# A new order for the first two batches of an attention and max-out kernel, and new PSUM bank rings

## The chip, the core and the metric

The kernel runs on one core of a Trainium2 chip, in one launch. The metric is device microseconds (us) from its start to its end; smaller is better. Times before: 151.38 us, the median of three runs (151.37 to 151.61).

## The reference

```python
# x (8, 8, 512, 64), state (8, 8, 32, 64); B, H, S, D and 32 state rows
a      = softmax(x @ state^T / 8, over the state rows)
xread  = a @ state
a2     = softmax(state @ x^T / 8, over the 512 tokens)
sread  = a2 @ x
t      = concat([xread, sread], axis=2) -> (8 * 544, 512)     # heads side by side
out    = max(t @ w1, t @ w2) @ w_out                           # 512 -> 1024 -> 512
```

All inputs and the output are float32 in DRAM; the kernel computes in bfloat16 with float32 sums in PSUM.

## The kernel before, in words

Rewriting. `max(h1, h2) = h2 + relu(h1 - h2)`, so with `wd = w1 - w2` the output is `t @ (w2 @ w_out) + relu(t @ wd) @ w_out`. The product `w2 @ w_out` is called `wwo`; the kernel makes it once (`wq`, from transposed `w2t`, which comes from `w2` steps, and `wo`). Since xread is `a @ state`, the state is multiplied into the weights first: `SW[b]` is the block-diagonal state (`sbd`) of batch b times `wd` (columns 0 to 1023, in pieces of 128 numbered 0 to 7) and times `wwo` (pieces 8 to 11). These products (`sw`, line 326) use the array in tiles of 64 rows by 32 columns. The attention weights, transposed (`aT`), are then multiplied with `SW`. The state reads (`sr`, line 296) use the array in tiles of 128 by 32. Everything else uses it whole. Going from one tiling to another is what "a change of tiling" means below.

Steps of one batch, by their names in the order: `ldx` loads x (two halves of 512 KB), `ce` casts it to bf16 (`xe`), `xt` transposes it on the array (later batches: `cb` casts to `xb`, and `xtd` transposes by DMA), `sc` gives the scores, their eviction is an exponential (`e`), `nmr` sums and inverts, `nmm` multiplies (`a`), `at` transposes `a` on the array (later `atd`, by DMA), `sr` and `srt` read the state side, `sw` makes `SW`, `l1.b.f` is the product with `wd`, evicted by a relu to `r` (eight pieces f), and the output of 128 tokens by 512 columns is summed from eight `l2p` products with `wo` and two `l2o` products with `aT`; `l2` is all ten together. `store` writes a batch (1 MB). `S` and `S7` transpose the state of batch 0 and of batches 1 to 7 into `sbd`. `cw2`, `cwo`, `sub` turn float32 weight pieces into bf16 `w2b`, `wo`, `wd`. `idle.n.512` are n products of zeros that only keep the array busy.

What sets the order. There is no scheduler at work: in manual schedule each engine runs its instructions in program order, and semaphores make it wait for data and for PSUM banks. The string `ORDER` at the top is that program order up to the end of batch 1 (with the first steps of batch 2). A token `name>V`, `>A`, `>P` is a step on DVE, ACT or POOL (with a digit before it: one half of the eviction), `name:k` is a step of TensorE into PSUM bank k (two digits for `sw`: two banks), and names without either are DMA issues on SP's queue, all of them in one row. Behind it a loop over b = 2 to 6 does, for batch b, the eight `l1`, the scores of batch b + 1, two output tiles, `SW` and `sr` of batch b + 1, and two more tiles; then a tail does batch 7, the 256 state-side tokens (`m1`, `m2`), and the last stores.

In the loop and the tail banks come from rings: `bank("r")` walks through six banks for products and scores, `bank("a")` through two for output tiles; in the tail ring a has all eight.

Staging. Float32 loads go into ten buffers of 1 MB (`h8`): `w1`, `w2`, `w_out` in two halves each, four batches of x; output tiles and later batches reuse them in turn. `xt`, `e`, `a`, `SW`, `r` have two buffers, `aT` three.

Of the kernel before, what the change touches and what calls it, by code (L numbers as in the profile page):

```python
# [45 lines left out]


# [1 line left out]
def kernel(  # L49
# [10 lines left out]
    B, H, S, D = x.shape  # L60
# [17 lines left out]
    at = ctx.enter_context(tc.tile_pool(name="at", bufs=2))  # L78
# [67 lines left out]
    def load_w(w, src, f, n):  # L146
        lo, hi = f * 128, (f + n) * 128
        h, o = lo // 512, lo // 512 * 512
        nc.sync.dma_start(out=half(w, h)[:, :, lo - o:hi - o], in_=src[:, lo:hi].rearrange("(i p) f -> p i f", p=128))  # L149
# [168 lines left out]
    def sw_mm(b, lo, hi, rings="rr"):  # L318
        if b not in SW:
            SW[b] = big.tile([128, 2, WC], BF16, tag="sw", name="sw")  # L320
        pg = [bank(r) for r in rings]
        n = hi - lo
        for i in range(4):
            for g in range(2):
                rhs = wd[64 * g:64 * g + 64, i, lo:hi] if hi <= FF else wwo[64 * g:64 * g + 64, i, lo - FF:hi - FF]
                nc.tensor.matmul(pg[g][32 * i:32 * i + 32, 0:n],  # L326
                                 sbd[64 * g:64 * g + 64, b, i, 32 * g:32 * g + 32], rhs, start=True, stop=True)
# [178 lines left out]
    def l2_mm(b, c, ring):  # L506
# [215 lines left out]
```

## Time and profile before

| | |
|---|---|
| median of three runs | 151.38 us |
| the profiled execution's own time | 151.53 us |
| its span (first to last instruction) | 149.7 us |
| busy: TensorE, DVE, ACT, POOL | 141.2, 80.9, 72.3, 49.8 us |
| DMA | 29.08 MB, mean 194 GB/s; some 11 MB of it are the loads of weights, state and four batches that the order begins with |
| end of the written order on TensorE | 55.57 us after the span's start |
| one batch in the loop | 13.85 us |

A row of the profile in order of time has the start and length in us, the engine, the line, the operation, the tiles written and read, the shape, the count, and, in brackets, how long the engine was idle before it and what ended that. PE is TensorE, DVE VectorE, ACT ScalarE, POOL GpSimd, SPq the queue from which DMAs are issued. The chain of waits follows back from the last instruction what released each step.

### The profile page before, as it was taken

The numbers are of one execution on the slowest core, as the hardware profiler recorded it, in microseconds if no ns is written. First come the engines' busy times: TensorE is split into PE (matmuls) and PEld (weight loads), VectorE is DVE, ScalarE is ACT, GpSimd is POOL, SyncE is SP. The second block draws the span as 40 slices with busy tenths as digits, with TensorE's granted clock in tenths as the row PEclk, the third lists the DMA queues.
The fourth block names the chain that finished last, engine by engine and source line by source line (L and its number), as shares of the span: only waits on it lengthen the run. The fifth ranks groups of instructions, "written<-read, shape, count | busy, mean of one in ns | idle before, by whom it ended". The sixth has DMA issues, their size and how long they took to land.

```text
span 149.7 us, 3138 instructions
## 1 busy us (share of the span) xinstructions
PE 141.2 (94%) x1253; PEld 69.2 (46%) x1253; DVE 80.9 (54%) x164; ACT 72.3 (48%) x140; POOL 49.8 (33%) x73
## 2 busy tenths in 40 slices
PE   6698999898999999999999999999999999999990
PEld 2354454353454445444534454454445444754460
DVE  4369364578676108663757385467627485632100
ACT  4298766655899217153713644072537045510121
POOL 3135210483995032652392349055600500000000
PEclk9999999999999999999999999999999999999999
DMA  3999999999207998776949586977306072102442
GB/s 77 364 363 362 359 366 265 328 348 210 54 4 142 235 344 315 162 155 224 311 91 264 223 236 115 273 292 142 74 0 280 0 208 103 44 0 74 118 167 78
DMA packets 35374, 29.08 MB, mean 194 GB/s; under 512 B 19900, under 2 KB 32444, under 8 KB 34588
## 3 DMA queue, kind: packets, MB, share of 16 engines
q1 hardware_dynamic: 35356, 28.84, 65.4%
q8 instruction: 11, 0.18, 0.6%
q14 instruction: 7, 0.06, 0.2%
HBM read 15.20 MB, written 8.91 MB: 161 GB/s over the span
## 4 chain that ended last, share of the span: by engine, by line
PE 75%; DMA 9%; SPq 5%; issue 5%; DVE 3%; POOL 1%; ACT 1%; ACTq 0%; POOLq 0%
PE bank L371 31%; PE bank L353 17%; PE bank L366 8%; DMA h<-in_moe_w_dram 8%; PE bank L326 4%; PE bank L498 3%; SPq L149 3%; PE bank L400 2%; PE bank L410 2%; PE bank L247 2%; PE bank L296 2%; DVE sbd L101 1%; SPq L153 1%; DMA out_dram<-h 1%; PE bank L408 1%
## 5 line engine op out<-in xcount | busy, mean ns | idle before, releaser
L371 PE MATMUL bank<-wo,r 128*128 128x512 bf16 (+1 forms) x232 | 53.1, 372 | 0.0
L99 ACT COPY h<-bank 128x512 f32<-128x512 f32 (+1 forms) x19 | 10.8, 569 | 51.0 <-PE bank L371 50.9
L371 PEld LDWEIGHTS <-r 128*128 128x128 bf16 x232 | 22.7, 98 | 25.7
L353 PE MATMUL bank<-aT,sw 128*128 128x512 bf16 x128 | 29.9, 379 | 0.0
L344 DVE TENSOR_SCALAR r<-bank 128x512 bf16<-128x512 f32 x28 | 19.2, 690 | 14.6 <-PE bank L353 13.2
L265 POOL TENSOR_TENSOR a<-e,er 128x512 bf16<-128x512 bf16 (+1 forms) x17 | 16.3, 980 | 26.5 <-ACT e L255 14.2
L342 ACT ACTIVATE r<-bank 128x512 bf16<-128x512 f32 x36 | 21.1, 605 | 7.2 <-PE bank L353 6.8
L101 DVE CAST sw<-bank 128x512 bf16<-128x512 f32 (+1 forms) x22 | 13.5, 649 | 12.5 <-PE bank L326 12.4
L103 POOL CAST xb<-h 128x1024 bf16<-128x1024 f32 x12 | 12.4, 1040 | 22.7 <-issue 15.6
L103 POOL CAST xe<-h 128x512 bf16<-128x512 f32 x26 | 15.0, 613 | 11.7 <-DMA h<-in_x_dram 11.5
L353 PEld LDWEIGHTS <-sw 128*128 128x128 bf16 x128 | 11.9, 98 | 13.6 <-issue 0.5
L366 PE MATMUL bank<-sw,aT 128*128 128x512 bf16 (+1 forms) x58 | 16.9, 373 | 0.0
L99 ACT CAST sw<-bank 128x512 bf16<-128x512 f32 (+1 forms) x30 | 15.4, 574 | 2.8 <-PE bank L326 2.8
L101 DVE COPY h<-bank 128x512 f32<-128x512 f32 x14 | 9.4, 668 | 12.7 <-PE bank L371 12.1
L261 DVE TENSOR_REDUCE sums<-e 128x16 f32<-128x512 bf16 (+1 forms) x18 | 10.9, 604 | 3.1 <-ACT e L255 3.0
L255 ACT ACTIVATE e<-bank 128x512 bf16<-128x512 f32 (+1 forms) x18 | 9.4, 549 | 3.6 <-PE bank L247 3.0
L498 PE MATMUL bank<-wo,r 128*128 128x512 bf16 x32 | 8.9, 380 | 0.0
L445 PE MATMUL bank<-wo,w2t 128*128 128x512 bf16 x32 | 8.1, 380 | 0.0
L453 PE MATMUL bank<-wz 128*128 128x512 bf16 x14 | 6.6, 558 | 1.2 <-DVE ones L457 1.2
L326 PE MATMUL bank<-wd,sbd 64*32 64x512 bf16 (+1 forms) x144 | 6.0, 359 | 1.2 <-DVE wd L434 1.2
L247 PEld LDWEIGHTS <-xt 128*128 128x128 bf16 x128 | 5.4, 101 | 3.3 <-ACT xt L99 0.6
L366 PEld LDWEIGHTS <-aT 128*128 128x128 bf16 x58 | 4.9, 98 | 4.1
(80 smaller groups left out, 118.2 us busy)
## 6 DMA issues: line engine op xcount, KB each, us to landing
h<-in_x_dram SPq DMA_DIRECT2D x16, 512.0 KB, 6.7
out_dram<-h SPq DMA_DIRECT2D x6, 1024.0 KB, 4.2
h<-in_moe_w_dram SPq DMA_DIRECT2D x8, 512.0 KB, 10.0
h<-in_moe_w_out_dram SPq DMA_DIRECT2D x4, 512.0 KB, 10.6
out_dram<-h SPq DMA_DIRECT2D x2, 512.0 KB, 3.8
out_dram<-h SPq DMA_DIRECT2D x3, 256.0 KB, 2.1
out_dram<-rs SPq DMA_DIRECT2D x8, 64.0 KB, 1.7
sf<-in_state_dram SPq DMA_DIRECT2D x2, 224.0 KB
```

Of the source, the lines that this page charges most:

```text
L99: nc.scalar.copy(o, i)
L101: nc.vector.tensor_copy(o, i)
L103: nc.gpsimd.tensor_copy(o, i)
L261: nc.vector.tensor_reduce(s_, e_view(b, k0, kn), axis=AXX, op=ALU.add)
L265: (nc.gpsimd if eng == "P" else nc.vector).tensor_mul(e_view(b, k0, kn, "a"), e_view(b, k0, kn), d_(b)["er"][:, :, k0:k0 + kn].unsqueeze(3 ...
L326: nc.tensor.matmul(pg[g][32 * i:32 * i + 32, 0:n], sbd[64 * g:64 * g + 64, b, i, 32 * g:32 * g + 32], rhs, start=True, stop=True)
L342: recent["A"] = nc.scalar.activation(out=o, in_=p, func=ACTF.Relu)
L344: nc.vector.tensor_scalar(o, p, scalar1=0.0, scalar2=None, op0=ALU.max)
L353: nc.tensor.matmul(p, SW[b][:, g, f * 128:(f + 1) * 128], AT[b][:, g].rearrange("p c t -> p (c t)"), start=(g == 0), stop=(g == 1))
L366: nc.tensor.matmul(p[:, lo:hi], AT[b][:, g, c, :], SW[b][:, g, FF + lo:FF + hi], start=(start and g == 0), stop=(stop and g == 1))
L371: nc.tensor.matmul(p[:, lo:hi], R[b][:, f, c * 128:(c + 1) * 128], wo[:, f, lo:hi], start=(start and j == 0), stop=(stop and j == len(fs) ...
L498: nc.tensor.matmul(p, R[b][:, j, c * 128:(c + 1) * 128], wo[:, j, :], start=first(key), stop=last(key, j == f + n - 1))
```

## The change

It has three parts. First, `ORDER` is another one: the same steps, with one product more among the idle ones (15 in place of 14), in another sequence on each engine, with other engines for some evictions and casts, and other banks. The loads start with x of batch 0 and then the state; of the weights the pieces 6 and 7 come ahead of 2 to 5, and `w1` 2 and 3 last; x of batch 1 follows `S7`. On the array `S7` and batch 1's `xt` stand later, `sw` groups stand next to each other more often, and `sr.1` next to `sr.2`. `store.0` is issued ahead of `xtd.3`. Second, ring r is banks 5, 7, 6, 1, 2, 4 and ring a is 3, 0. Third, in the tail ring a is the old ring a followed by ring r, written as a sum.

```diff
--- before.py
+++ after.py
@@ -16,32 +16,32 @@
 
 
 ORDER = """
-ldS.0.1 ldx.0.1 ldx.0.0 ldw2.0.2 ldw1.0.2 ldwo.0.2 ldw2.2.2 ldw1.2.2 ldwo.2.2 ldw2.6.2 ldw2.4.2 ldwo.6.2
-ldwo.4.2 ldw1.4.2 ldx.1.1 ldS7 ldx.1.0 ldw1.6.2 ldx.2.1 ldx.2.0 ldx.3.1 ldx.3.0 idle.4.512:0 cS.0.1>V S.0.1:0
-idle.3.512:1 S.0.1>0V S.0.1>1A ce.0.2>V ce.0.3>A xt.0.2.1:1 xt.0.3.1:2 xt.0.2.1>V idle.1.512:3 xt.0.3.1>V
-sc.0.2.1:3 sc.0.2.1>A sc.0.3.1:4 idle.1.512:5 ce.0.1>P ce.0.0>A nmr.0.2.1>V sc.0.3.1>A xt.0.1.1:5 xt.0.0.1:6
-nmr.0.3.1>V xt.0.1.1>A idle.1.512:7 xt.0.0.1>A nmm.0.2.1>V nmm.0.3.1>P sc.0.1.1:7 sc.0.1.1>A sc.0.0.1:0
-idle.1.512:1 nmr.0.1.1>V sc.0.0.1>A cw2.0.1>P cw2.1.1>A sr.0:1 nmr.0.0.1>V nmm.0.1.1>P w2.0.2:2 sr.0>V
-idle.1.512:3 nmm.0.0.1>P w2.0.2>A sub.1.1>V srt.0:3 at.0.0:4 at.0.1:5 at.0.0>A idle.2.512:6 sub.0.1>V
-cwo.0.1>A cwo.1.1>P at.0.1>V sw.0.0.2:67 srt.0>A wq.1.0.2:0 sw.0.0.2>0A sw.0.0.2>1V wq.2.0.2:1 cw2.2.1>V
-cw2.3.1>A l1.0.0:2 l1.0.1:4 l1.0.0>A w2.2.2:5 l1.0.1>A wq.0.0.2:3 sub.2.1>V w2.2.2>A l2p.0.3.0.2:6 sub.3.1>V
-l2p.0.2.0.2:7 wq.3.0.2:2 cwo.2.1>P cwo.3.1>A sw.0.2.2:45 wq.0.2.2 sw.0.2.2>0V sw.0.2.2>1A wq.2.2.2 cw2.7.1>A
-l1.0.2:5 l1.0.3:4 cw2.6.1>A l1.0.2>V wq.1.2.2 l1.0.3>A wq.3.2.2 cw2.4.1>P cw2.5.1>V w2.6.2:5 l2p.0.3.2.2
-w2.6.2>V w2.4.2:4 cwo.7.1>A l2p.0.2.2.2 cwo.6.1>V w2.4.2>A l2p.0.1.0.2:5 wq.2.6.2 cwo.4.1>V cwo.5.1>A wq.0.6.2
-l2p.0.1.2.2 wq.2.4.2 wq.3.6.2 sub.4.1>V wq.2>A wq.0.4.2 sub.5.1>V wq.1.4.2 wq.0>A wq.1.6.2 ce.1.2>P ce.1.3>A
-wq.3.4.2 wq.1>V sw.0.4.2:41 wq.3>A xt.1.2.2:3 sw.0.4.2>1A l2p.0.0.0.2:0 cS7>P xt.1.2.2>V sw.0.4.2>0A
-sw.0.8.4:21 l1.0.5:4 sw.0.8.4>0A l2p.0.0.2.2 ce.1.1>V l1.0.5>A S7:3 ce.1.0>V sw.0.8.4>1A l1.0.4:2 S7>0V
-xt.1.0.2:4 l1.0.4>V l2o.0.2 sub.7.1>P xt.1.0.2>A l2o.0.3 S7>1V l2o.0.0 l2o.0.1 sub.6.1>V ce.2.3>P sc.1.0.2:1
-sc.1.2.2:2 sc.1.0.2>A sw.0.6.2:43 cb.2.1>P l2p.0.1.4.2 sw.0.6.2>0A sw.0.6.2>1V l2p.0.0.4.2 sc.1.2.2>A
-nmr.1.0.2>V sw.1.0.4:14 cb.2.0>P sr.1:3 sw.1.0.4>0A nmr.1.2.2>V l1.0.7:2 nmm.1.0.2>P xtd.2 l1.0.6:1 l1.0.7>A
-sr.1>V l2p.0.3.4.2 l1.0.6>A l2p.0.2.4.2 nmm.1.2.2>P sw.1.0.4>1V sw.1.4.4:23 srt.1:1 l2p.0.3.6.2 sw.1.4.4>0A
-sw.1.4.4>1V ce.3.0>P at.1.1:4 l2o.0.3>A l2p.0.0.6.2 ce.3.2>P at.1.0:2 at.1.1>A l2o.0.0>V l2p.0.2.6.2 ce.2.2>P
-srt.1>A sw.1.8.4:36 ce.3.3>P l2o.0.2>A at.1.0>V sw.2.0.4:41 sw.1.8.4>1V sw.1.8.4>0A ce.2.0>P l1.1.5:0
-sw.2.0.4>0A l1.1.0:2 ce.2.1>P l1.1.5>V sw.2.0.4>1A l1.1.1:7 cb.3.1>P sc.2.0.2:3 l1.1.0>V l1.1.1>A l1.1.2:6
-sc.2.2.2:4 sc.2.0.2>A ce.3.1>P l1.1.4:0 l1.1.2>A l1.1.7:1 cb.3.0>P nmr.2.0.2>V sc.2.2.2>A l1.1.6:2 l1.1.3:7
-l1.1.4>A nmr.2.2.2>V nmm.2.0.2>P xtd.3 sr.2:3 l1.1.6>A sw.2.4.4:64 l1.1.3>A sr.2>V nmm.2.2.2>P sw.2.8.4:02
-l1.1.7>A l2p.0.1.6.2 sw.2.4.4>0V sw.2.8.4>1A srt.2:7 l2.1.2:3 l2o.0.1>A atd.2 ldx.4.0 ldx.4.1 srt.2>V
-sw.2.8.4>0A sw.2.4.4>1A store.0 l2.1.1:1 l2.1.2>A l2.1.0:2 l2.1.1>V l2.1.3:6 l2.1.0>A l2.1.3>V store.1
+ldx.0.1 ldS.0.1 ldx.0.0 ldw2.0.2 ldwo.0.2 ldw1.0.2 ldw2.6.2 ldwo.6.2 ldw1.6.2 ldw2.2.2 ldwo.2.2 ldw2.4.2
+ldwo.4.2 ldw1.4.2 ldS7 ldw1.2.2 ldx.1.0 ldx.1.1 ldx.2.0 ldx.2.1 ldx.3.0 ldx.3.1 idle.11.512:0 ce.0.2>V
+ce.0.3>A cS.0.1>P xt.0.2.1:0 S.0.1:1 xt.0.3.1:2 xt.0.2.1>V S.0.1>1A idle.1.512:3 S.0.1>0A xt.0.3.1>V
+sc.0.2.1:3 sc.0.3.1:4 sc.0.2.1>A idle.1.512:5 sc.0.3.1>A ce.0.0>P ce.0.1>V nmr.0.2.1>V xt.0.1.1:5 xt.0.1.1>A
+xt.0.0.1:6 nmr.0.3.1>V nmm.0.2.1>P cw2.1.1>A sc.0.1.1:7 cw2.0.1>P xt.0.0.1>V sc.0.1.1>A sc.0.0.1:0 nmm.0.3.1>P
+w2.0.2:1 nmr.0.1.1>V sc.0.0.1>A cwo.0.1>P cwo.1.1>A sr.0:2 nmr.0.0.1>V w2.0.2>A nmm.0.1.1>P idle.2.512:3
+sr.0>V nmm.0.0.1>P wq.0.0.2:3 sub.1.1>V at.0.1:4 srt.0:5 at.0.0:6 at.0.1>A sub.0.1>V wq.2.0.2:7 wq.3.0.2:0
+cw2.7.1>A cw2.6.1>V sw.0.0.2:12 at.0.0>A srt.0>V w2.6.2:4 sw.0.0.2>1V sw.0.0.2>0A wq.1.0.2:5 cwo.7.1>P
+w2.6.2>V l1.0.0:6 cwo.6.1>P l1.0.1:2 l1.0.0>A wq.3.6.2 l1.0.1>A sub.7.1>V wq.2.6.2 wq.1.6.2 sub.6.1>V
+l2p.0.2.0.2:1 sw.0.6.2:46 cw2.2.1>V cw2.3.1>A wq.0.6.2 sw.0.6.2>0V sw.0.6.2>1A w2.2.2:2 l1.0.7:6 cwo.2.1>A
+w2.2.2>V l1.0.6:4 cwo.3.1>A l1.0.7>V l2p.0.1.0.2:2 l1.0.6>A wq.1.2.2 cw2.4.1>P cw2.5.1>A wq.3.2.2 wq.2.2.2
+w2.4.2:6 cwo.4.1>P l2p.0.1.6.2 w2.4.2>V l2p.0.2.6.2 cwo.5.1>P wq.0.2.2 wq.0.4.2 sub.4.1>V sub.5.1>P wq.1.4.2
+wq.0>A wq.3.4.2 wq.2.4.2 wq.3>A l2p.0.0.0.2:4 wq.1>V wq.2>A l2p.0.0.6.2 cS7>P sw.0.4.2:63 sw.0.8.4:07
+sw.0.4.2>0V sw.0.4.2>1A l2p.0.3.0.2:5 sw.0.8.4>0A l2p.0.3.6.2 sub.3.1>V sw.0.8.4>1A S7:3 l1.0.4:6 sub.2.1>V
+S7>0A l2o.0.0 S7>1V l2o.0.2 ce.1.1>P l1.0.4>A l2o.0.3 sw.0.2.2:07 ce.1.0>V sw.1.4.4:63 sw.0.2.2>0A l2o.0.1
+sw.0.2.2>1V ce.1.3>P sw.1.4.4>0A xt.1.0.2:0 sw.1.4.4>1A ce.1.2>P l1.0.2:7 xt.1.0.2>V l1.0.3:6 l1.0.2>A
+xt.1.2.2:3 ce.2.1>P l1.0.3>A sc.1.0.2:0 cb.2.0>P xt.1.2.2>V l1.0.5:7 sc.1.0.2>A l2p.0.3.2.2 l1.0.5>A
+sc.1.2.2:6 nmr.1.0.2>V cb.2.1>P l2p.0.1.2.2 sc.1.2.2>A l2p.0.0.4.2 l2p.0.2.2.2 nmr.1.2.2>V nmm.1.0.2>P xtd.2
+l2p.0.0.2.2 l2p.0.2.4.2 nmm.1.2.2>V l2o.0.0>A ce.3.0>P l2p.0.1.4.2 l2o.0.2>A l2p.0.3.4.2 l2o.0.1>A at.1.1:3
+ce.3.3>P at.1.0:0 at.1.1>A sw.1.8.4:76 ce.3.1>P at.1.0>V sw.1.0.4:41 l2o.0.3>A sw.1.8.4>1V sw.2.8.4:23
+ce.2.2>P l1.1.6:0 sw.1.0.4>1A store.0 cb.3.1>P l1.1.4:5 sw.1.0.4>0V sw.2.8.4>0A l1.1.7:6 sw.2.8.4>1A l1.1.4>V
+l1.1.0:1 ce.2.3>P l1.1.7>A l1.1.1:4 l1.1.6>V ce.2.0>P sw.1.8.4>0A l1.1.3:2 l1.1.0>V sc.2.0.2:3 ce.3.2>P
+l1.1.3>A sc.2.2.2:5 l1.1.5:6 l1.1.1>V cb.3.0>P sc.2.2.2>A l1.1.2:0 sc.2.0.2>A l1.1.5>V sw.2.0.4:71 l1.1.2>A
+xtd.3 sw.2.4.4:24 sr.2:5 nmr.2.0.2>V sw.2.0.4>1A sr.1:3 l2.1.0:6 sw.2.4.4>1A sr.1>V nmm.2.0.2>P nmr.2.2.2>V
+srt.1:0 l2.1.2:1 sr.2>V nmm.2.2.2>P srt.1>A sw.2.0.4>0V atd.2 ldx.4.0 ldx.4.1 l2.1.0>V srt.2:4 l2.1.1:3
+sw.2.4.4>0V l2.1.2>A srt.2>A l2.1.3:0 l2.1.1>A l2.1.3>V store.1
 """
 
 
@@ -82,7 +82,7 @@
 
 
     banks = [psum.tile([128, 512], F32, name=f"bank{i}") for i in range(8)]
-    rings = {"r": [0, 1, 2, 3, 4, 5], "a": [6, 7]}
+    rings = {"r": [5, 7, 6, 1, 2, 4], "a": [3, 0]}
     turn = {"r": 0, "a": 0}
 
     def bank(ring="r", dtype=F32):
@@ -597,7 +597,7 @@
             store(b)
 
     b = B - 1
-    rings["a"] = [6, 7, 0, 1, 2, 3, 4, 5]
+    rings["a"] = rings["a"] + rings["r"]
     turn["a"] = 0
     for f in range(NF):
         l1(b, f)
```

## The prediction

> **What bounds the kernel now.** I read the page first, then the chain of waits, then TensorE's rows in order of time.
>
> ```profile
> span 149.7 us, 3138 instructions
> PE 141.2 (94%) x1253; PEld 69.2 (46%) x1253; DVE 80.9 (54%) x164; ACT 72.3 (48%) x140; POOL 49.8 (33%) x73
> PE   6698999898999999999999999999999999999990
> ...
> DMA  3999999999207998776949586977306072102442
> 21.40:55.60 34.20, 32.72 (x331) 15.79 (x329) 19.69 (x38) 21.70 (x41) 16.48 (x20) 1.00 0.81 217
> 55.60:69.40 13.80, 13.80 (x130) 6.42 (x129) 8.87 (x17) 5.53 (x10) 5.33 (x7) 1.00 0.81 230
> 55.57 3.62 PE L353 MATMUL bank<-aT,sw 128*128 128x512 bf16 x16
> ...
> 69.42 3.62 PE L353 MATMUL bank<-aT,sw 128*128 128x512 bf16 x16
> ```
>
> The page gives TensorE 94% of the span. The stretch rows (stretch; then busy time of PE, weight load, DVE, ACT, POOL; clock; DMA) show it busy without a gap from 55.6 us on, with every other engine well under it: a batch begins at 55.57 and the next at 69.42, 13.85 us later. So the steady loop and the tail can change only if the array does other work there, and it does not. Everything turns on when the hand-written order ends, which is the 55.57 of the row (its last output tile, then the loop's first product). In the first 25 us the DMA engines are full: there, the loads decide.
>
> The profiled execution took 151.53 us with a span of 149.7, so 1.83 lie around it; the median of the runs is 151.38, 0.15 less. I sum against the span.
>
> **The change part by part.** *The stretch that counts.* I walked both orders step by step with durations of the rows below, and looked for a point behind which the array has the same work left. Before, at 21.42 (the step `l2p.0.3.2.2`) what is left in the order is 116 products of 512 columns, one `w2` group, two `sw` groups of 256 columns and seven of 512, `S7`, two `xt`, four `sc`, two `at`, two `sr`, two `srt`. In the new order exactly this list is left from `wq.1.2.2` on. So that step and the old 21.42 can be compared directly: old cost of the list 55.57 - 21.42 = 34.15 us.
>
> ```profile
> 21.42 0.59 PE L498 MATMUL bank<-wo,r 128*128 128x512 bf16 x2
> ...
> 27.14 0.30 PE L326 MATMUL bank<-wd,sbd 64*32 64x256 bf16 x8
> 27.86 0.62 PE L229 MATMUL bank<-ident,xe 128*128 128x128 bf16 x8 [0.42 <-POOL xe L103]
> ...
> 31.33 1.89 PE L504 MATMUL bank<-sw,aT 128*128 128x512 bf16 x8
> 33.51 0.63 PE L247 MATMUL bank<-sbd,xt 128*128 128x64 bf16 x16 [0.29 <-DVE sbd L101]
> 34.88 0.30 PE L326 MATMUL bank<-wd,sbd 64*32 64x256 bf16 x8 [0.74 <-DVE wd L434]
> 35.12 1.04 PE L498 MATMUL bank<-wo,r 128*128 128x512 bf16 x4
> 36.09 0.41 PE L326 MATMUL bank<-wd,sbd 64*32 64x512 bf16 x8
> 36.42 0.43 PE L296 MATMUL bank<-xe,e 128*32 128x65 bf16 x32
> ...
> 40.86 0.41 PE L326 MATMUL bank<-wwo,sbd 64*32 64x512 bf16 x8
> 41.09 0.40 PE L326 MATMUL bank<-wd,sbd 64*32 64x512 bf16 x8
> 41.51 1.46 PE L353 MATMUL bank<-aT,sw 128*128 128x512 bf16 x6
> ...
> 53.85 1.89 PE L371 MATMUL bank<-wo,r 128*128 128x512 bf16 x8
> ...
> 59.03 0.63 PE L247 MATMUL bank<-sbd,xt 128*128 128x64 bf16 x16
> 59.49 0.60 PE L366 MATMUL bank<-sw,aT 128*128 128x512 bf16 x2
> ```
>
> ```profile
> L371 PE MATMUL bank<-wo,r 128*128 128x512 bf16 (+1 forms) x232 | 53.1, 372 | 0.0
> ```
>
> Columns: start, length, engine, line, tiles, shape, count, and idle time with what ended it. From the eight products at 53.85 to the loop's first at 55.57 are 1.72 us, so one takes 0.2157 (the group of all of them shows 0.372 from start to end, since they overlap).
>
> *Waits that go.* At 27.14 a 256-column group starts; the like one at 34.88 is followed 0.24 later, so the next step could start at 27.38 and starts at 27.86, held by batch 1's x: 0.48. At 31.33 eight products need 1.73, to 33.06; the scores start at 33.51, held by the state matrices of batches 1 to 7: 0.45. The sixteen score products take 0.46 (59.03 to 59.49), so 33.97, plus 0.10 for the change of tiling below, 34.07; the group starts at 34.88, held by a subtraction: 0.81. Last, 41.09 plus the 0.33 of the row 36.09 to 36.42 is 41.42 against 41.51: 0.09. Together 1.83 us. The new order puts `xt.1.*` ten and fourteen products behind `S7`, takes `w1` 2/3 as the late weight instead of 6/7, and moves its `sub` in front of the S7 evictions. By my walk x of batch 1 is ready about 1 us, `sbd` 0.6 us, and `sub.2` about 1 us before the array asks. What is late next are evictions, below.
>
> *Changes of tiling.* A 512-column `sw` group followed by another of its kind takes 0.23 (40.86 to 41.09); followed by another tiling 0.33 (36.09 to 36.42); and entering costs 0.10 to 0.11 (35.12 plus four products is 35.98, the group starts at 36.09). So a change costs 0.10. From the compared point on the old order has 16 of them, the new one 9 (four islands of `sw`/`sr` in place of seven, with fewer turns inside): 7 times 0.10 is 0.70 us. The Trainium skill, "TensorEngine Tiling (Array Packing)", Key Properties, says a change of tiling mode drains the engine. A full drain would be, by the rows, what a product lasts beyond its 0.2157: 0.372 less 0.216, or 0.16, and 7 would give 1.1. The trace shows 0.10, which I use.
>
> ```profile
> 0.74 0.46 SPq L157
> ...
> 7.64 1.12 SPq L149
> 8.81 11.36 DMA h<-in_moe_w_dram
> h<-in_moe_w_dram SPq DMA_DIRECT2D x1, 512.0 KB, 11.0
> aT<-a SPq DMA_TRANSPOSE x6, 3.1
> 18.80 1.14 ACT L99 CAST w2b<-h 128x512 bf16<-128x512 f32 x2
> 15.70 1.02 POOL L103 CAST wo<-h 128x512 bf16<-128x512 f32 x1 [2.40 <-DMA h<-in_moe_w_out_dram]
> 24.95 1.29 DVE L434 TENSOR_TENSOR wd<-h,h 128x512 bf16<-128x512 f32 x2 [1.60 <-DMA h<-in_moe_w_dram]
> 33.49 1.34 DVE L434 TENSOR_TENSOR wd<-h,h 128x512 bf16<-128x512 f32 x1
> 32.26 2.02 POOL L103 CAST xb<-h 128x1024 bf16<-128x1024 f32 x2
> 9.40 0.38 DVE L265 TENSOR_TENSOR a<-e,er 128x256 bf16<-128x256 bf16 x1
> L103 POOL CAST xb<-h 128x1024 bf16<-128x1024 f32 x12 | 12.4, 1040 | 22.7 <-issue 15.6
> 43.63 1.04 POOL L103 CAST xb<-h 128x1024 bf16<-128x1024 f32 x1
> 30.30 1.27 POOL L434 TENSOR_TENSOR wd<-h,h 128x512 bf16<-128x512 f32 x1 [1.51 <-DMA h<-in_moe_w_dram]
> 47.41 1.23 SPq L277 DMA_TRANSPOSE aT<-a  x1
> ```
>
> *When the list starts.* `wq.1.2.2` needs `wo` 2 and 3, the tenth 512 KB load of the new order. The tenth of the old one landed at 8.81 + 11.36 = 20.17 (chain of waits). Bytes ahead are the same; x of batch 0 is issued 0.5 us earlier (S's issue, 0.46, goes behind its first half), but I take nothing for that. Two ACT casts follow (`cwo.2`, `cwo.3`): a pair takes 1.14 (row 18.80), and 0.1 for the hand-overs gives 21.4. The other way in: the ninth load, `w2` 2/3: the old ninth was issued at 7.64 and landed 11.0 later (the row of the DMA view for that issue), at 18.64; a cast 0.6, then `w2.2.2` (0.44) and three pairs of products (0.43 each) end at about 21.1. So the list starts at 21.4 again, and all earlier moves cost nothing while they fit under this: S behind x, `cS` on POOL, 15 filling products in place of 14 (11 of them in front of the first transposes), the other weights' order. Their cover is the array's own wait for the ninth load, some 1.2 us by my walk; beyond that they cost one for one.
>
> *Sum without new waits.* 21.4 + 34.15 - 1.83 - 0.70 = 53.0.
>
> *New waits.* The new order is tight at the evictions; many of its banks come free only 0.1 to 0.3 us before they are asked for. The places by rows: `sub.4` on DVE now runs beside `sub.5` on POOL. Alone the pair took 1.29 (0.65 each, row 24.95); beside POOL's casts one took 1.34 (33.49 against 32.26). The Trainium skill, "SBUF — State Buffer", Who interferes with whom, has a vector instruction with two SBUF inputs contend with POOL's reads; this pair of rows agrees, and the rule speaks against this change. The 0.69 falls ahead of `wq.1`'s eviction and `sw.0.8.4`, with 0.2 to 0.7 of room: 0 to 0.2 us lost. `nmm.1.2` goes from POOL to DVE, also two SBUF inputs beside POOL: half the size took 0.38 (row 9.40), so 0.75 alone and 1.5 if held up likewise; `at.1.1` then `l1.1.6` wait on it with 0.1 of room: 0 to 0.6. Together 0 to 0.8, plus small hand-overs; I take 0.5, since the old stretch too had only one wait under 0.1 beside its three large ones. Order's end: 53.5, against 55.57, **2.1 us earlier**.
>
> *Edits at nothing.* The bank rings: r was 0 to 5, a was 6, 7; now r is 5, 7, 6, 1, 2, 4 and a is 3, 0, and the tail's list is a followed by r in both. That is a renaming, place by place; only the first turn can differ, and there the loop has nothing to win since its array rows have no gaps. SP's queue: `store.0` now goes ahead of `xtd.3` and would hold it until batch 0's last eviction at about 39, but `xtd.3` waits anyway for POOL's cast of batch 3's `xb`, which ran at 43.63 and by my walk comes at about 43. `atd.2` was issued at 47.41 and such a transfer lands 3.1 later; the loop's first product asks at 53.5 instead of 55.57, so it is still covered by about 3 us; without cover it would cost one for one. POOL's last casts and products end at about 47 in both by my walk. From there each step of loop and tail shifts by the same 2.1 us.
>
> So the span is 147.6, the profiled time 149.4, and scaled to the median 149.3.
>
> **The rivals.**
> *B, more gain.* The loads stream earlier by the 0.5 us of x's issue, or no new wait shows: 0.5 to 0.8 less, 148.6. For: the page's DMA row is full from its second slice on. Against: nothing in the order was made looser.
> *C, half of it.* Evictions and softmax of batch 1 wait in turn, with 0.8 of the above and again 0.7 over a dozen places with 0.1 to 0.3 of room: 150.3. For: ACT and DVE are busy 21.7 and 19.7 of 34.2 us here, in bursts. Against: the old order had such places and lost 0.09.
> *D, nothing.* The tenth load lands 2 us later and the list starts at 23.4: 151.4. For: between the old eighth load, cast on arrival at 15.70, and the old ninth at 18.64 lie 2.9 us, where the tenth follows after 1.5, so landings are not even. Against: the tenth came at 20.17 all the same.
> *E, slower.* One mechanism: batch 1's softmax is late. Before, its x reached the array at 27.86 and its first product came at 41.51, 13.6 us later; now about 31.6 and 39.0, 7.4 us. The second half of x is now the sixteenth load, and the old sixteenth landed at 30.3 (POOL row 30.30). POOL then has casts and a product from 30.3 to about 36.4, 6 us; if DVE's work next to it stretches these by half, 3 us, `l1.1.6` is at 42 instead of 39, and the end at 56.0: 151.8. It decides from 2.1 us on beyond the new waits counted. For: the two rows of contention. Against: POOL's own casts keep their length beside DVE (32.26: 1.01 each, the mean over twelve is 1.04).
>
> *F, not what it says:* the steady banks change nothing, by the above; that lies within the forecast.
>
> **How the numbers follow.** Forecast 149.3 (its own range 148.8 to 149.9): 0.50. B 0.13, C 0.20, D 0.06, E 0.11. A measurement here tells about 0.2%, 0.3 us, from no change. Faster: forecast, B and C, 0.83; same: D, 0.06; slower: E, 0.11. The range goes from 148.5 (all of B but its far end) to 151.0 (all of C with its spread): D and E, 0.17, and some of B are left out.
>
> **What would show it.** In the changed profile: the array's first loop product (L353, sixteen products) at 53.5 instead of 55.57, later batches still 13.85 apart and the same tail behind it. `wq.1.2.2` (L445) at about 21.4, led by the landing of `wo` 2/3. No array row with over 0.3 us of idle time behind 21.4; `sw` rows standing in four islands, 0.23 apart inside, 0.33 at the end. DVE's `wd` row near 25 us at about 1.3 for one. Wrong: a wait over 0.5 us behind 21.4, most of all before the `at` transposes (L283) or the first `l1.1` products; a list start off by more than 0.5; or a loop that begins with a gap because `aT` of batch 2 lands later than 53.

## The result, and the profile after

The changed kernel takes 150.19 us (median of 15 runs, 148.89 to 151.62), the one before 151.37 (15 runs, 150.55 to 151.82); the ratio is 0.9922, with a 95% interval of 0.9893 to 0.9951. That is 1.2 us or 0.8% faster, in the direction forecast, and little more than half of the 2.1 us forecast. Medians here and below are of all runs, while ratios and intervals leave out the runs that took over 1.5% longer than the fastest of the same kernel (in e11 these are six of twelve).

The profiled execution took 150.07 us. Its span was 148.3 us. These are rows of TensorE in order of time (start, length, what, idle time and what ended it), rows of DVE and POOL beside them, and one row of the chain of waits.

```profile
18.70 0.30 PE L326 MATMUL bank<-wd,sbd 64*32 64x256 bf16 x8 [1.10 <-DVE wd L434]
...
21.27 1.46 PE L445 MATMUL bank<-wo,w2t 128*128 128x512 bf16 x6
...
26.18 1.03 PE L498 MATMUL bank<-wo,r 128*128 128x512 bf16 x4
27.36 0.30 PE L326 MATMUL bank<-wd,sbd 64*32 64x256 bf16 x8
27.48 0.88 PE L326 MATMUL bank<-wwo,sbd 64*32 64x512 bf16 x8
28.29 1.04 PE L498 MATMUL bank<-wo,r 128*128 128x512 bf16 x4
...
31.38 0.86 PE L326 MATMUL bank<-wd,sbd 64*32 64x256 bf16 x16
32.18 0.61 PE L504 MATMUL bank<-sw,aT 128*128 128x512 bf16 x2
...
54.11 3.62 PE L353 MATMUL bank<-aT,sw 128*128 128x512 bf16 x16
67.96 3.62 PE L353 MATMUL bank<-aT,sw 128*128 128x512 bf16 x16
```

```profile
13.78 11.63 DMA h<-in_moe_w_dram
25.51 1.79 DVE L434 TENSOR_TENSOR wd<-h,h 128x512 bf16<-128x512 f32 x1 [1.60 <-DMA h<-in_moe_w_dram]
27.22 0.68 DVE L101 CAST wwo<-bank 128x512 bf16<-128x512 f32 x1
30.69 1.09 DVE L101 COPY sbd<-bank 64x896 bf16<-64x896 bf16 x1 [0.85 <-ACT sbd L99]
25.49 1.27 POOL L434 TENSOR_TENSOR wd<-h,h 128x512 bf16<-128x512 f32 x1 [0.86 <-DMA h<-in_moe_w_dram]
```

The order ends at 54.11 instead of 55.57, 1.46 us earlier, and a turn of the loop takes 13.85 us as before (67.96 less 54.11). So all of the difference lies in the written order. The list of equal work starts at 21.27 (`wq.1.2.2`, the six L445 products; 21.4 was forecast) and takes 54.11 - 21.27 = 32.84 us, in place of 34.15.

Where it waits, by the starts: four products from 26.18 end at 27.04, plus 0.10 for the change of tiling, and `sw.0.4.2` starts at 27.36: 0.22 late. `sw.0.8.4` starts at 27.48 and its successor at 28.29, 0.81 instead of 0.33: 0.48 late. `sw.0.2.2` and `sw.1.4.4` from 31.38 should be through after 0.12 + 0.33 and are after 0.80: 0.35 late. With 0.11 at a group near 40 (39.71 to 40.15, where 0.33 would do) this makes about 1.15 us of new waits. Without them the list would take 31.69; the forecast without new waits was 34.15 - 1.83 - 0.70 = 31.62.

The second fence names the first two. The load of `w1` 4/5, the thirteenth, is issued at 13.78 and lands at 25.41. `sub.4` on DVE and `sub.5` on POOL start together, and `sub.4` takes 1.79 us; behind it, `wq.1`'s eviction ends at 27.90, and `sw.0.8.4` needs it. The third wait is for the second eviction of `S7`, on DVE, which sat idle for 0.85 us until ACT's eviction had ended. Both read one bank and write `sbd`; which of the two the semaphore was for, the profile does not say.

### The profile page after: what moved, and what is told of

The parts are those of the page before. It is cut to its first block, busy times and chain, and to the rows that moved or that the text cites. A ratio compares the mean times of both kernels' runs of the same rounds, so it can differ in the third digit from the quotient of the medians.

```text
span 148.3 us, 3150 instructions
## 1 busy us (share of the span) xinstructions
PE 140.8 (95%) x1254; PEld 68.7 (46%) x1254; DVE 82.3 (56%) x164; ACT 68.1 (46%) x134; POOL 53.7 (36%) x79
## 4 chain that ended last, share of the span: by engine, by line
PE 77%; DMA 9%; SPq 8%; DVE 2%; issue 1%; ACT 1%; DVEq 0%; ACTq 0%
PE bank L371 31%; PE bank L353 18%; PE bank L366 8%; DMA h<-in_moe_w_dram 8%; PE bank L326 4%; SPq L149 4%; SPq L153 4%; PE bank L498 3%; PE bank L400 2%; PE bank L410 2%; PE bank L247 2%; PE bank L296 2%; DMA out_dram<-h 1%; PE bank L504 1%; DVE wd L434 1%; PE bank L408 1%
## 5 line engine op out<-in xcount | busy, mean ns | idle before, releaser
L371 PEld LDWEIGHTS <-r 128*128 128x128 bf16 x232 | 22.7, 98 | 25.7
L344 DVE TENSOR_SCALAR r<-bank 128x512 bf16<-128x512 f32 x30 | 20.4, 690 | 13.9 <-PE bank L353 13.2
L342 ACT ACTIVATE r<-bank 128x512 bf16<-128x512 f32 x34 | 20.1, 598 | 7.5 <-PE bank L353 7.1
L103 POOL CAST xb<-h 128x1024 bf16<-128x1024 f32 x12 | 12.6, 1058 | 21.3 <-issue 20.1
L103 POOL CAST xe<-h 128x512 bf16<-128x512 f32 x28 | 17.2, 651 | 3.2 <-DMA h<-in_x_dram 3.2
L99 ACT CAST sw<-bank 128x512 bf16<-128x512 f32 (+1 forms) x29 | 14.8, 574 | 1.8 <-PE bank L326 1.8
L101 DVE COPY h<-bank 128x512 f32<-128x512 f32 x13 | 8.7, 666 | 9.4 <-PE bank L371 9.4
L445 PE MATMUL bank<-wo,w2t 128*128 128x512 bf16 x32 | 8.2, 379 | 0.4 <-ACT w2t L99 0.4
L434 DVE TENSOR_TENSOR wd<-h,h 128x512 bf16<-128x512 f32 x7 | 6.3, 929 | 3.9 <-DMA h<-in_moe_w_dram 3.9
L498 PE MATMUL bank<-wo,r 128*128 128x512 bf16 x32 | 8.1, 379 | 0.0
```

The source lines that it names most:

```text
L99: nc.scalar.copy(o, i)
L101: nc.vector.tensor_copy(o, i)
L103: nc.gpsimd.tensor_copy(o, i)
L371: nc.tensor.matmul(p[:, lo:hi], R[b][:, f, c * 128:(c + 1) * 128], wo[:, f, lo:hi], start=(start and j == 0), stop=(stop and j == len(fs) ...
L498: nc.tensor.matmul(p, R[b][:, j, c * 128:(c + 1) * 128], wo[:, j, :], start=first(key), stop=last(key, j == f + n - 1))
```

## The experiments

The theory after this reading: the end of the new order hangs on the landing of `w1` 4/5 and on what follows it, and not on the tenth load that the prediction followed. The rival: the start of the list at 21.3 sets the end, and the waits are small things on the way. The landing of loads moves from profile to profile, and the times of the changed kernel spread over 2.7 us, so most verdicts below rest on distances inside a profile, and the medians stand beside them. Where a row counts fewer products than the sixteen or eight of its step, records are missing or the view ended there; the starts used here are not touched by that.

**The changed kernel again (e0).**

> The changed kernel again, unaltered, beside the variants. Theory: the list of work behind wq.1.2.2 begins near 21.3 us and the order ends at 54.1 us with three waits in between (0.2 and 0.5 us around sub.4 beside sub.5, 0.35 us at the second eviction of S7), so about 150.2 us, 0.8% under the kernel before; only the landing of the loads moves from run to run, and with it the start of the list by up to 0.5 us. Rival: the difference is drift of the loads alone; then the order's end lies above 55 us in this profile.

149.69 us, ratio 0.9928 (0.9894 to 0.9962). The profile's chain and order's end:

```profile
14.09 10.62 DMA h<-in_moe_w_dram
24.80 1.79 DVE L434 TENSOR_TENSOR wd<-h,h 128x512 bf16<-128x512 f32 x1 [1.67 <-DMA h<-in_moe_w_dram]
53.41 3.62 PE L353 MATMUL bank<-aT,sw 128*128 128x512 bf16 x15
```

The load lands at 24.71 and the order ends at 53.41. In the first profile it was 25.41 and 54.11. The distance is 28.70 us in both. `sub.4` takes 1.79 again. The list starts at 20.50 here, 0.77 earlier than in the first profile, so these two profiles alone would fit the rival too (32.91 and 32.84 us from the start of the list).

**The load of `w1` 4/5 later (e11).**

```diff
-ldwo.4.2 ldw1.4.2 ldS7 ldw1.2.2
+ldwo.4.2 ldS7 ldw1.4.2 ldw1.2.2
```

> The two S7 loads (448 KB) go ahead of the load of w1 4/5. Theory (in the changed kernel the order's end hangs on that load: in five profiles 28.70 us from its landing, which varied from 24.7 to 25.7): it lands some 1.2 us later, the distance stays 28.7, and the kernel takes 1.2 us more, about 151.2 us. Rival (the start of the list at 21.3 sets the end, as the prediction summed it): no change in the end, or the 0.4 us by which w1's chain then exceeds its cover.

```profile
16.50 10.13 DMA h<-in_moe_w_dram
55.33 2.97 PE L353 MATMUL bank<-aT,sw 128*128 128x512 bf16 x12
```

It lands at 26.63, 1.2 us later than in the first profile; the order ends at 55.33: again 28.70. From the start of the list (21.24) it is 34.09 us here, against 32.84 in the first profile and 33.43 in e5, so that distance is not the constant one. The time is 152.0 us, ratio 0.9985 (0.9941 to 1.0029), by the ratios about 0.6% or 0.9 us more than the unaltered kernel's; the two intervals overlap, so the times alone would not decide. In the profile the theory holds, to the hundredth.

Over e0, e4, e5, e6 and the first profile the landing moves from 24.71 to 25.73, and the distance stays 28.69 to 28.70 (in e4 to the end of the last eight products, since the loop starts late there). The three of these executions that differ in nothing behind the landing (e0, the first, e6) took 149.30, 150.07 and 150.40 us with landings at 24.71, 25.41 and 25.73: the time follows the landing nearly one for one. That the whole spread of the runs without a profile comes from this load is likely, but not shown.

**The kernel before again (e10).** No edit.

> The kernel before, unaltered, for a second profile. Theory: its order's end hangs on the landing of x 4 to 7 of batch 1 (27.1 us), from which to the end of the order are 28.4 us; that distance stays within 0.1 us whatever the landing is, the three waits (x, state, subtraction) are there again, and a loop turn takes 13.85 us. Rival: the three waits come and go from run to run.

```profile
27.19 0.61 POOL L103 CAST xe<-h 128x512 bf16<-128x512 f32 x1 [6.35 <-DMA h<-in_x_dram]
26.63 0.62 POOL L103 CAST xe<-h 128x512 bf16<-128x512 f32 x1 [6.13 <-DMA h<-in_x_dram]
32.96 0.63 PE L247 MATMUL bank<-sbd,xt 128*128 128x64 bf16 x16 [0.29 <-DVE sbd L101]
34.33 0.30 PE L326 MATMUL bank<-wd,sbd 64*32 64x256 bf16 x8 [0.75 <-DVE wd L434]
55.02 3.19 PE L353 MATMUL bank<-aT,sw 128*128 128x512 bf16 x13
```

150.91 us. The first row is the first profile's. POOL casts batch 1's x as it lands, at 27.19 there and at 26.63 here; the order ends at 55.57 and at 55.02: 28.38 and 28.39 us later. The two other waits are there with the same lengths, 0.29 and 0.75. The wait for x itself is not: it shrinks from 0.48 to 0.11, since the array came to it 0.19 earlier and x 0.56 earlier, and with it the list takes 55.02 - 21.23 = 33.79 us instead of 34.15. The chain of waits of this profile leads back to that load, which landed at 26.58. So, by two profiles and without a run that moves the load, the old order hung on its fourteenth load; the new one hangs on its thirteenth, and the difference of the two first profiles is that of the landings, with what follows: POOL's step on the arrived data began at 27.19 before and begins at 25.49 now, 1.70 us earlier, and the way from there is 54.11 - 25.49 = 28.62 instead of 28.38, 0.24 longer: 1.46.

**`wo` 2/3 later (e7).**

```diff
-ldw2.2.2 ldwo.2.2 ldw2.4.2
+ldw2.2.2 ldw2.4.2 ldwo.2.2
```

> The loads w2 4/5 and w_out 2/3 change places, so that wo 2/3 comes eleventh instead of tenth. Theory (the tenth load sets when the list of work starts): wo 2/3 lands some 1.4 us later, wq.1.2.2 starts at about 22.7 instead of 21.3, and the order ends 1.4 us later: +1.4 us. Rival (the start is set by the array's own work, or the later loads set the end): under 0.3 us.

```profile
11.28 9.37 DMA h<-in_moe_w_out_dram
21.34 1.76 PE L445 MATMUL bank<-wo,w2t 128*128 128x512 bf16 x6 [0.96 <-ACT wo L99]
24.60 1.79 DVE L434 TENSOR_TENSOR wd<-h,h 128x512 bf16<-128x512 f32 x1 [0.33 <-DMA h<-in_moe_w_dram]
26.40 1.03 PE L498 MATMUL bank<-wo,r 128*128 128x512 bf16 x4
27.36 0.30 PE L326 MATMUL bank<-wd,sbd 64*32 64x256 bf16 x8
53.64 3.62 PE L353 MATMUL bank<-aT,sw 128*128 128x512 bf16 x15
```

150.61 us, ratio 0.9962 (0.993 to 0.9995), against 0.9928 unaltered: not told apart, and not the 1.4 us of that theory. But all loads came early in this profile: the load lands at 20.65, only some 0.45 later than in the first one, and the list starts at 21.34, so the 22.7 of the theory never arose. What the profile does give is distances. The array waits for the load, 0.96 by the row, and the wait ahead of `sw.0.4.2` is gone (four products from 26.40 and 0.10 make 27.36, its start). `sub.4` begins at 24.60, so `w1` 4/5 landed at about 24.51 (0.09 before it, as in e0), and by its 28.70 the order would end at 53.21; it ends at 53.64, and the chain of waits begins at `wo` 2/3. So in this run the exchanged load was the longer way, by 0.43 us: more than the rival allowed, and far less than the theory. From its landing to the end are 32.99 us. With 20.2 for it in the first profile (ACT's casts of `wo` start at 20.21 there) that way would end at 53.2, 0.9 us before the way over `w1` 4/5. This is the term that the prediction had built on, and in the changed kernel it was not the longest.

**Two more filling products (e6).**

```diff
-idle.11.512:0
+idle.13.512:0
```

> 13 filling products at the start in place of 11. Theory: the early part has about 1.1 us of room, since the array waits for the subtractions of w1 6/7 at 18.7 us anyway; two products of 0.43 us move the first transposes from 5.84 to 6.7 us, and the start of the list at 21.3 and the order's end stay: no change. Rival (the softmax of batch 0 is on the path): +0.85 us.

```profile
18.88 0.30 PE L326 MATMUL bank<-wd,sbd 64*32 64x256 bf16 x8 [0.48 <-DVE wd L434]
13.84 11.89 DMA h<-in_moe_w_dram
54.42 3.62 PE L353 MATMUL bank<-aT,sw 128*128 128x512 bf16 x15
```

The wait for the subtractions of `w1` 6/7 (1.10 us at 18.70 in the changed kernel, first fence) shrinks to 0.48 and the distance from the landing (25.73) is 28.69: the two products are covered, in the profile. The times, 150.52 us, ratio 0.9958 (0.9929 to 0.9986), overlap with the unaltered kernel's and cannot show it.

**Both subtractions on DVE (e1, and again as e9).**

```diff
-sub.4.1>V sub.5.1>P
+sub.4.1>V sub.5.1>V
```

> sub.5 goes back from POOL to DVE, behind sub.4. Theory (contention: sub.4 took 1.79 us beside sub.5 on POOL): sub.4 now takes 0.65 us and sub.5 ends at about 26.8 us, or 27.4 if the S7 cast on POOL slows it in turn; wq.1's eviction then ends 0 to 0.4 us earlier than now (27.90), and the order ends 0 to 0.4 us earlier. Rival (sub.4 was long for another reason, such as its late load): sub.4 stays at about 1.8 us, the pair ends at 28, and the order ends 0.6 us later.

> The kernel of e1 again (both subtractions on DVE), whose profile and times disagreed: from the landing of w1 4/5 to the order's end it took 29.50 us where the changed kernel takes 28.70, but its median time was the lower one. Theory (the contention only moves to POOL's S7 cast, and the pair on DVE is 0.4 us later): again over 28.9 us from that landing, and about 150.2 us with the usual landing. Rival (the move helps): under 28.5 us, and 149.3 us.

```profile
13.78 12.08 DMA h<-in_moe_w_dram
25.95 2.16 DVE L434 TENSOR_TENSOR wd<-h,h 128x512 bf16<-128x512 f32 x2 [1.89 <-DMA h<-in_moe_w_dram]
25.93 1.04 POOL L103 CAST sb<-sf 112x1024 bf16<-112x1024 f32 x1 [0.67 <-DMA sf<-in_state_dram]
55.36 3.62 PE L353 MATMUL bank<-aT,sw 128*128 128x512 bf16 x15
```

```profile
14.41 10.84 DMA h<-in_moe_w_dram
25.34 1.29 DVE L434 TENSOR_TENSOR wd<-h,h 128x512 bf16<-128x512 f32 x2 [1.76 <-DMA h<-in_moe_w_dram]
27.10 1.04 POOL L103 CAST sb<-sf 112x1024 bf16<-112x1024 f32 x1 [2.93 <-DMA sf<-in_state_dram]
53.45 3.62 PE L353 MATMUL bank<-aT,sw 128*128 128x512 bf16 x15
```

The same kernel, two profiles. In the first POOL casts the state for `S7` at the moment of the subtractions, the pair takes 2.16 us, and from the landing to the order's end are 55.36 - 25.86 = 29.50. In the second that cast comes at 27.10, after them; the pair takes 1.29, and the distance is 53.45 - 25.25 = 28.20. My expectation for e1 missed: the pair was through at 28.11, and not by 27.4, and the end came 0.80 later, near the rival's 0.6, but by POOL's cast and not by a late load. My expectation for e9 (over 28.9 again) missed as well: the rival's distance (under 28.5) came, its time of 149.3 did not. The profiled execution of e1 was the slowest of its seven, 151.26 us against a median of 149.31, so its profile need not be the usual case. The medians are 149.31 and 150.17, the ratios 0.9885 (0.9858 to 0.9912) and 0.992 (0.9886 to 0.9953): whether this edit gains on average stays open.

So what holds up a subtraction on DVE is POOL work that began before it, a cast as well as a subtraction. By the rows the subtraction then ends 0.54 or 0.55 us after that work: in the changed kernel POOL is through at 25.49 + 1.27 = 26.76 and `sub.4` at 25.51 + 1.79 = 27.30; in the kernel before, POOL's two casts are through at 32.26 + 2.02 = 34.28 and the subtraction at 33.49 + 1.34 = 34.83. So 1.34 and 1.79 are not two prices for two kinds of work; they say how long POOL still had to run.

The Trainium skill, "SBUF — State Buffer", Who interferes with whom, has a vector instruction with two SBUF inputs contend with POOL's reads, and says that who issued first decides who is held up. The lengths of a subtraction on DVE agree: 0.65 alone, 1.34 beside casts, 1.79 when POOL's own subtraction began 0.02 us earlier. That a port is the cause no run here shows.

**One product pair ahead of the `sw` island (e2).**

```diff
-l2o.0.3 sw.0.2.2:07 ce.1.0>V sw.1.4.4:63 sw.0.2.2>0A l2o.0.1
+l2o.0.3 l2o.0.1 sw.0.2.2:07 ce.1.0>V sw.1.4.4:63 sw.0.2.2>0A
```

> l2o.0.1 moves ahead of sw.0.2.2 and sw.1.4.4, nothing else. Theory (sw.1.4.4 waits for the second S7 eviction, because DVE may read the bank only when ACT has read it): 0.43 us of products now cover 0.35 us of wait, and the order ends 0.35 us earlier, about 149.9 us. Rival (DVE's eviction was late on its own, behind the subtractions, or the wait turns up at the next transposes): no change.

```profile
32.41 0.52 PE L326 MATMUL bank<-wd,sbd 64*32 64x256 bf16 x16
33.20 0.61 PE L229 MATMUL bank<-ident,xe 128*128 128x128 bf16 x8 [0.27 <-ACT sw L99]
```

149.98 us, ratio 0.9929: no change. The wait inside the island is gone (sixteen products in 0.52 instead of 0.86), but the next transposes come at 33.20 where 32.41 + 0.45 would be 32.86: they wait 0.34 for bank 0, until ACT has evicted `sw.0.2.2`. That wait, too, had been there and was covered by the pair that I moved. From the landing of `w1` 4/5 (26.02) to the order's end (54.69) are 28.67 us, 0.03 less. The rival was right.

**Three moves (e3), and a cover for the fourth wait (e8).** In e3, beside the edit of e2:

```diff
-wq.0.4.2 sub.4.1>V sub.5.1>P wq.1.4.2 ... wq.1>V wq.2>A
+wq.0.4.2 sub.5.1>P wq.1.4.2 ... wq.1>V sub.4.1>V wq.2>A
-sw.0.4.2:63 sw.0.8.4:07
+sw.0.8.4:07 sw.0.4.2:63
```

and in e8 further:

```diff
-sw.0.8.4>0A l2p.0.3.6.2 sub.3.1>V
+sw.0.8.4>0A sub.3.1>V
-sw.1.4.4>0A xt.1.0.2:0
+sw.1.4.4>0A l2p.0.3.6.2 xt.1.0.2:0
```

> The move of e2, and in addition wq.1's eviction goes ahead of sub.4 on DVE and sw.0.8.4 ahead of sw.0.4.2 on the array, so that the first sw group of the island no longer needs sub.4. Theory: of the 0.69 us lost there about 0.2 to 0.3 stay (sub.4 ends near 27.4 to 27.8), of the 0.35 nothing; the order ends at 53.3 to 53.5 us, 0.6 to 0.8 us earlier than in the changed kernel, about 149.5 us. Rival (the evictions behind are the bound, and the array waits somewhere else for what it no longer waits for here): less than 0.3 us.

> The three moves of e3, and l2p.0.3.6.2 goes from ahead of S7 to between sw.1.4.4 and xt.1.0.2. Theory: in e3 the first transposes of batch 1 wait 0.34 us for bank 0 until ACT has evicted sw.0.2.2; two products (0.43 us) cover that, S7 itself starts 0.43 us earlier, and the order takes 0.34 us less from the start of the list: 31.9 instead of 32.2 us, in time 0.3 us less than e3 (149.1), so about 148.8, 1.4% under the kernel before. Rival (the eviction ahead of it on ACT is late for another reason): the wait stays, 149.1.

```profile
20.90 1.46 PE L445 MATMUL bank<-wo,w2t 128*128 128x512 bf16 x6
26.71 0.41 PE L326 MATMUL bank<-wwo,sbd 64*32 64x512 bf16 x8
27.09 0.30 PE L326 MATMUL bank<-wd,sbd 64*32 64x256 bf16 x8
53.12 3.62 PE L353 MATMUL bank<-aT,sw 128*128 128x512 bf16 x15
```

```profile
20.43 1.46 PE L445 MATMUL bank<-wo,w2t 128*128 128x512 bf16 x6
13.44 11.18 DMA h<-in_moe_w_dram
30.62 0.60 PE L498 MATMUL bank<-wo,r 128*128 128x512 bf16 x2
31.07 0.62 PE L229 MATMUL bank<-ident,xe 128*128 128x128 bf16 x8
52.57 3.62 PE L353 MATMUL bank<-aT,sw 128*128 128x512 bf16 x15
```

e3 takes 149.08 us, ratio 0.9879 (0.9842 to 0.9915); its list takes 53.12 - 20.90 = 32.22 us, 0.62 less than 32.84, and of the island's 0.70 only 0.15 is left (27.09 instead of 26.94). The chain of waits no longer runs over `w1` 4/5: it leads back through the wait for bank 0 and the array's own work to `w1` 6/7, which landed at 16.97. With the waits behind `sub.4` gone, the start of the list is the next thing that counts.

e8 takes 148.76 us, ratio 0.9856 (0.9827 to 0.9886), its runs within 148.54 to 149.56. The wait for bank 0 is covered: the transposes follow `l2p.0.3.6.2` after 0.45. Its list takes 32.14, not the 31.9 expected: `S7`, now earlier, waits about 0.2 for its cast on POOL, which stands behind `sub.5` there. From the landing of `w1` 4/5 (24.62) to the end are 27.95 us, 0.75 less than in the changed kernel. That the median came out at the 148.8 expected is luck: of the 0.55 us between the ends of e3 and e8, 0.47 is an earlier start of the list and only 0.08 the list itself. The two are not told apart, since their intervals overlap; e8's lies wholly below that of the unaltered changed kernel in e0, and e3's overlaps with it.

**The old bank rings (e4).**

```diff
-rings = {"r": [5, 7, 6, 1, 2, 4], "a": [3, 0]}
+rings = {"r": [0, 1, 2, 3, 4, 5], "a": [6, 7]}
```

> The changed order with the old bank rings (r 0 to 5, a 6 and 7). Theory: only the first turn differs; the loop's first product then asks for bank 0, which holds batch 1's last output tile until its eviction ends at about 55.1 us, so the loop starts about 0.95 us later than 54.1, and everything behind it: +0.95 us. Later batches stay 13.85 us apart. Rival (a renaming throughout, as the prediction had it): no change. A second rival (the new rings also help inside the loop): more than 13.85 us per batch.

```profile
52.69 1.89 PE L371 MATMUL bank<-wo,r 128*128 128x512 bf16 x8
55.43 3.61 PE L353 MATMUL bank<-aT,sw 128*128 128x512 bf16 x15 [0.85 <-DVE h L101]
69.28 3.62 PE L353 MATMUL bank<-aT,sw 128*128 128x512 bf16 x16
```

The last eight products from 52.69 are through at 54.42; the loop starts at 55.43, 1.01 us late, with 0.85 of it shown as idle behind DVE's eviction of the last output tile from bank 0. The next turn is 13.85 us later, as always. The time is 150.88 us, ratio 0.9981 (0.9949 to 1.0014). So by the profile the new rings are worth about 1.0 us with the new order: they bring nothing over the old kernel, but keep the new order from losing most of its gain at the seam. The times agree with that, though the interval still overlaps with that of the unaltered kernel.

**`sw` groups apart in the loop (e5).**

```diff
-        l2(b, 1)
-        pg = [sw_mm(n, 512 * z, 512 * z + 512) for z in range(3)]
+        pa = bank("a")
+        pg = [sw_mm(n, 0, 512)]
+        l2_open(b, 1, pa, True, False)
+        pg.append(sw_mm(n, 512, 1024))
+        l2_f(b, 1, pa, range(NF), False, True)
+        pg.append(sw_mm(n, 1024, 1536))
+        l2_out(b, 1, pa, "A")
```

> In the loop's five turns the three sw groups no longer stand together: the two parts of the second output tile stand between them, so that one island of other tiling becomes three, four changes of tiling more in a turn. Theory (0.10 us for a change): a batch takes 13.85 + 0.40 = 14.25 us and the kernel 2.0 us more. By the Trainium skill, TensorEngine Tiling (Array Packing), Key Properties, the array drains at each; at the 0.16 us that a product lasts beyond its turn that would be 0.64 a batch and 3.2 us more. Rival (changes cost nothing where weights are loaded ahead; the 0.10 was something else): no change.

```profile
54.35 3.62 PE L353 MATMUL bank<-aT,sw 128*128 128x512 bf16 x15
68.68 2.54 PE L353 MATMUL bank<-aT,sw 128*128 128x512 bf16 x11
```

A turn takes 14.33 us in place of 13.85: 0.48 for four changes of tiling, 0.12 each. 152.32 us, ratio 1.0075 (1.0042 to 1.0107), which is 2.2 us over the unaltered kernel's 0.9928. That is the 0.10 of the rows with a little on top, and below the 0.16 estimated for a full drain. So the seven changes saved are worth 0.7 to 0.85 us of the array's time.

## Why the prediction was right, and where it was off

*The end of the order decides, loop and tail shift along*: right. 13.85 us a turn, the same tail, and 1.46 us at the order's end in the profile.

*The list starts at 21.4, behind the tenth load*: the start was right (21.27), in part by luck. In the first profile the array comes to it from its wait at 18.70 for the subtractions of `w1` 6/7, with only 0.15 us of idle time on the way; the casts of `wo` 2/3 ended at 21.35, just in time, and did not lead it. Nor did the tenth load set the end (e7): that way had some 0.9 us of room.

*Waits that go, 1.83 us, and seven changes of tiling, 0.70*: right together, 31.62 us forecast for the list without new waits, 31.69 in the rows; the price of a change, 0.10, was 0.12 by itself (e5).

*New waits, 0.5 us*: this is the term that was mis-sized. They came to 1.15. For `sub.4` beside `sub.5` the text had 0 to 0.2 us lost, by rows in which the subtractions start at 24.95 and one of them takes 1.34. `sub.4` started at 25.51 and took 1.79, so it ended 1.01 us later than by those rows, and 0.70 of it reached the array. The second eviction of `S7`, 0.35, was not seen: the walk let ACT and DVE read the bank at once, and in the trace DVE waited for ACT. `nmm.1.2` beside POOL, for which up to 0.6 was put in, cost nothing: it ran in 0.69 us. It began at 37.55, 0.01 us ahead of POOL's next cast, so it does not show what it would have taken behind one. So of the two places named by the contention rows one was worse and one was free. Under E the text also took POOL's casts to keep their length beside DVE; the state's cast for `S7` did not, with 1.50 us at 26.70, while `sub.4` still ran, and 1.04 in both profiles of e1's kernel.

```profile
37.55 0.69 DVE L265 TENSOR_TENSOR a<-e,er 128x512 bf16<-128x512 bf16 x1
```

The terms add up: 0.13 less at the start, 0.07 more for the list without new waits and 0.65 more for the new waits make the 0.6 us between 53.5 and 54.11. Of the signs, "no array row with over 0.3 us of idle time" did not hold (0.48 and 0.35); the places that were thought the likeliest, ahead of `at` and of the first `l1.1`, lost 0.11 at most.

*The rings at nothing*: right for this change, but the reason given was half of it; "only the first turn can differ" is where 1.0 us would have been lost (e4).

*Edits at nothing ahead of the list*: shown for the filling products (e6). For the others it was not tried.

*Half the gain (rival C)* came nearest: 150.3 was its time, by evictions that wait, though its dozen small places were two large ones. The forecast's own range, 148.8 to 149.9, missed the median by 0.3. What a single profile could not tell, and the text did not allow for, is that the thirteenth load lands anywhere between 24.6 and 26.0 us in the ten profiles that keep its place, and the order's end with it. The text took a measurement as good to 0.3 us; the interval of the result is about 0.45 us to either side.

## What to carry to other kernels

Where an order is written by hand and starts on a full DMA queue, follow from each late load forward to the end, and take the longest of these ways: a wait that is removed from one only uncovers the next. A distance from a landing to the end that stays the same in several profiles points to the load, when the run times are too scattered to tell; moving that one load in the queue settles it. A step on one engine beside another engine's work is to be costed with the length it has there, and in the rows here that depended on which of the two began first.

## What was not expected of the hardware

A subtraction of two SBUF operands on DVE took 0.65 us alone, 1.34 beside casts on POOL and 1.79 beside a subtraction on POOL, and in both slowed cases ended 0.54 or 0.55 us after the POOL work that had begun before it; a bf16 product of two SBUF operands on DVE that began 0.01 us ahead of a cast on POOL was not slowed (0.69 us). The thirteenth of the first loads landed between 24.62 and 26.02 us in the ten profiles that kept the first thirteen in place, and the state's load for `S7` landed before or after the subtractions in the same kernel (casts at 25.93 and 27.10).
